# A routed MLP on one core: three transposes a slot instead of four, and list, table and list-load work in another order

## Chip, core and metric

The kernel runs on one core of one Trainium2 chip. The metric is device time in microseconds (us), the median of three runs. The profile is that of one further execution.

## The reference, cut to what matters

`x` has 8 x 2880 tokens of 192 channels. A causal convolution of 7 taps (softmaxed, one row of taps for each of 8 heads) is followed by a two-level top-1 mixture of experts with 4 x 4 = 16 experts:

```python
out = np.einsum('hk,bskhg->bshg', w, x_unf)       # the convolution
g_idx = np.argmax(x @ w_group, axis=1)            # then, for each group g:
e_idx = np.argmax(xg @ w_expert[g], axis=1)
h  = np.maximum(xg[mask_e] @ w1[g, e], 0.0)       # 192 -> 1024
ye = h @ w2[g, e]                                 # 1024 -> 192
out[tok_idx] = (g_w * e_w)[:, None] * ye          # product of the two gates
```

## The kernel before

**Units.** The 23040 tokens are convolved and routed in 18 units of 4 to 12 blocks of 120 tokens. `unit(u)` is a generator that yields between small steps. It convolves (TensorE, then ScalarE copies), turns the result, makes logits, picks the expert on VectorE, and stores gate and convolved row (193 floats) to the DRAM table `xcd`; that store is issued from ScalarE's queue (line 532). Then it builds the lists of token numbers by expert: two halves of six blocks, each with the VectorE instructions `ohl` (L567), `ohr` (L571), `ohv` (L575), then small matmuls (L589), and a scatter by GpSimd into `idtab` (L601).

**Slots.** The experts' work is a list `plan` of 98 slots of up to 256 tokens. Portion 0 is one slot for each of 16 experts (slots 0 to 15, from the first 5 units), portions 1 and 2 are two slots for each expert (16 to 47 and 48 to 79), and the tail is 18 slots whose expert is read from a table computed on the chip, nine of two tiles of 128 tokens and nine of one, in turn. For each slot two indirect DMAs of GpSimd gather rows of `xcd` into one of four buffers `xg` (L673). `turn` turns them on TensorE into the PSUM tile `px` (L686: the first 128 channels of a tile; L687: the last 64), and ScalarE and VectorE split them into a high and a low part (`xa` L688 and L689, `xb` L692 and L693). `hidden` and `back` are the two matrix products, four steps `f2` in a slot of two tiles (L704; L722 and L726), with `hh` (L709) and `hl` (L710) between them. `finish` scales the sums in the two PSUM tiles `po` into `ys` (L784, L785) and GpSimd scatters them to the output (L775). Between steps of a slot `advance` takes steps of the units.

**Order.** Each engine's order is made by a scheduler when the kernel is built. It takes an instruction as soon as its own model of time has it ready, and so far ahead of its place in the program, unless `tc.keep_in_program_order` holds it. `open_slot(i)` is called at step 0 of slot i-2; `turn` for slot i at step 1 of slot i-1 (at step 0 if that slot has one tile). `open_portion` issues the 16 loads of token lists `idp` (L1017) of a portion from the SyncE queue at once. The arithmetic of the tail's table (`table`, L824 to L907) stands at slot 52 and after in the program, one piece for each `open_slot`, then one `idpt` list load (L1035) for each. In the tail, GpSimd also does one subtraction of each expert's weights (`bl`, L647).

Of the kernel before, what the change touches and what calls it, by code (L numbers as in the profile page):

```python
# [36 lines left out]
def conv_moe_kernel(  # L37
# [18 lines left out]
    PINW = True  # L56

# [79 lines left out]
    KPRE = [2, 150, 155, 160, 162, 20]  # L137
    CEU = 0
# [226 lines left out]
    xg = [const.tile([P, 2, XW], F32, name=f"xg{i}") for i in range(NXG)]  # L365
# [10 lines left out]
    def unit(u, pre=None):  # L376
# [155 lines left out]
        SE.dma_start(out=xcw, in_=xc[0:BT, 0:nb, 0:XW])  # L532
# [28 lines left out]
        for b0 in range(0, nb, HB2):  # L561
            n = min(HB2, nb - b0)
            ohl = pa.tile([P, HB2, P], F16, name="ohl", bufs=2)
            ohr = rt.tile([P, HB2, LH], F16, name="ohr", bufs=1)
            ohv5 = pa.tile([P, HB2, LH], F16, name="ohv", bufs=2)
            bs = slice(b0, b0 + n)
            nc.vector.tensor_tensor(  # L567
                out=ohl[0:Q, 0:n], in0=iop[0:Q].unsqueeze(1).broadcast_to([Q, n, P]), in1=bc(posb[0:Q, 0, bs], P),
                op=ALU.is_equal,
            )  # L570
            nc.vector.tensor_tensor(  # L571
                out=ohr[0:Q, 0:n], in0=ior[0:Q].unsqueeze(1).broadcast_to([Q, n, LH]), in1=bc(posb[0:Q, 1, bs], LH),
                op=ALU.is_equal,
            )
            OHE.tensor_tensor(  # L575
                out=ohv5[0:Q, 0:n], in0=ohr[0:Q, 0:n], in1=bc(vals[0:Q, bs], LH), op=ALU.mult)
            halves.append((b0, n, ohl, ohv5))
# [91 lines left out]
    def gather(ids, known, n=2):  # L669
        xs = xg[nslot[0] % NXG]  # L670
        nslot[0] += 1
        for t in range(n):
            nc.gpsimd.indirect_dma_start(  # L673
                out=xs[:, t, :], out_offset=None, in_=xcd[0:known, :],
                in_offset=bass.IndirectOffsetOnAxis(ap=ids[:, t, 0:1].bitcast(U32), axis=0),
                bounds_check=known - 1, oob_is_err=False,
            )
        return xs

    def turn(xs, n=2):  # L680
# [127 lines left out]

    def table(first=None, nbig=NBIG, nsmall=NSMALL):
# [10 lines left out]
        v = nc.vector  # L820
# [23 lines left out]
        v.memset(t["one"], 1.0)  # L844
        base = cons if first is None else first
        tt(t["rem"], ends[:, nends[0]], base, ALU.subtract)
        if first is None:
# [9 lines left out]
            tt(most, most, flags[:, 0:1], ALU.max)  # L857
            ts(flags[:, 0:1], most, float(SLOT), ALU.is_gt)
            ts(flags[:, 1:2], most, float(SLOT), ALU.is_le)
            ts(t["rem"], t["rem"], flags[:, 1:2], ALU.mult)  # L860
        slots(t["nf"], P - 1 if first is None else SLOT - 1)
        slots(t["ns"], SLOT - 1)
        tt(t["ns"], t["ns"], t["nf"], ALU.subtract)
        for n, pe, st in (("nf", "pa", "sa"), ("ns", "pb", "sb")):
# [6 lines left out]

        ts(c["m1"], c["j"], float(nbig), ALU.is_ge)
# [3 lines left out]
        stt(c["ja"], c["k"], -1024.0, c["ja"], ALU.mult, ALU.add)  # L876
        stt(c["k"], c["j"], -float(ntail), c["oa"], ALU.add, ALU.is_lt)
        stt(c["k"], c["k"], 1024.0, c["oa"], ALU.mult, ALU.add)
        tt(c["k"], c["k"], c["m2"], ALU.mult)
        stt(c["jb"], c["j"], -float(nbig), c["k"], ALU.add, ALU.subtract)  # L880
        for st, pe, j, m in (("sa", "pa", "ja", "ma"), ("sb", "pb", "jb", "mb")):
# [8 lines left out]
        v.tensor_reduce(out=c["k"], in_=t["q"], axis=AX.X, op=ALU.add)  # L890
        ts(ent[:, 0:1], c["k"], float(D), ALU.mult)
        ts(ent[:, 1:2], c["k"], float(F), ALU.mult)

        ts(c["ja"], c["ja"], float(SLOT), ALU.mult, -float(DUMMY), ALU.add)
        stt(t["q"], t["sa"], -float(SLOT), base, ALU.mult, ALU.add)
        stt(t["q"], t["q"], c["ja"], t["ma"], ALU.add, ALU.mult)
        stt(t["r"], t["nf"], float(SLOT), base, ALU.mult, ALU.add)
        stt(t["r"], t["r"], -float(DUMMY), t["mb"], ALU.add, ALU.mult)
        tt(t["q"], t["q"], t["r"], ALU.add)
# [27 lines left out]
    def stages(u):  # L927
        q = units[u][1] // QB
        return 1 + 8 + (2 * FRH if u >= FRU else 0) + sum(gaps(u)) + 3 * q + 1 + (LISTLAG if u >= NEED else 0)
# [69 lines left out]

    def open_portion(pi):  # L1000
# [9 lines left out]
        else:  # L1010
# [5 lines left out]
            for e in range(E):  # L1016
                nc.sync.dma_start(  # L1017
                    out=idp[:, e],
                    in_=idtab[bass.ds(base[e], P * rows), :].rearrange("(p r) c -> p r c", r=rows),
                )  # L1020
# [42 lines left out]
    def open_slot(i):  # L1063
# [49 lines left out]
    for k in range(AHEAD):  # L1113
        step()
    while opened[0][0]["todo"]:
        split_one(opened[0][0])
    unit_banks[:] = [(pm, "pm")]
    lead[:] = SKEW2, LIVE2
    turned[0] = turn(gathered[0])
# [13 lines left out]
    for i, (pi, e, s) in enumerate(plan):  # L1133
# [7 lines left out]
        for f2 in range(steps):  # L1141
# [25 lines left out]
            if f2 == 0:  # L1167
                open_slot(i + 2)
            for q in range(f2, NF // 2, steps):
# [101 lines left out]
```

## Time and profile before

| | |
|---|---|
| median of 3 runs | 1166.22 us (1163.81 to 1169.93) |
| the profiled execution | 1157.9 us, span 1156.1 us from first to last instruction |
| granted TensorE clock, mean | 0.991 |
| TensorE (PE) busy | 1105.5 us, 96% |
| VectorE (DVE) busy | 804.7 us, 70% |
| ScalarE (ACT) busy | 689.2 us, 60% |
| GpSimd (POOL) busy | 494.2 us, 43% |

Busy times of PE are unions of pipelined matmuls: each record is longer than the distance to the next start, so the cost of one is read from starts, not from its duration. The first transposes of the slots start at 97.31 us; those that run within slot 16 (the first with the change) start at 328.66 us, within slot 48 at 686.89 us, within slot 80 (the first of the tail) at 999.80 us.

### The profile page before, as it was taken

Reading aid. Unit: us, or ns where it says so; the run is one execution under the profiler, and the core shown is the slowest. Engines: PE = TensorE matmul, PEld = TensorE weight load, DVE = VectorE, ACT = ScalarE, POOL = GpSimd, SP = SyncE. Lnnn points to the kernel's source line nnn. Section 1 sums busy time; section 2 is a strip of 40 time slices with the busy share of each in tenths; the row PEclk is TensorE's granted clock in tenths of the full one; section 3 lists DMA queues with packets and bytes.
Section 4 is the critical chain, followed back from the end, with each engine's and each line's share of the span. In section 5 each row is a group of like instructions: output and inputs, shape, how many; then the busy total and the mean of one; then the engine's idle time right before and its main releaser. Section 6 shows DMA issues by size and latency. Waiting matters only on the chain.

```text
span 1156.1 us, 23806 instructions
## 1 busy us (share of the span) xinstructions
PE 1105.5 (96%) x8468; PEld 1076.4 (93%) x8468; DVE 804.7 (70%) x1668; ACT 689.2 (60%) x1374; POOL 494.2 (43%) x443
## 2 busy tenths in 40 slices
PE   6887999989999999999999999999999999999996
PEld 5777999989999999999998999999999999989986
DVE  4777788877867666666678565666666666688874
ACT  5474666657565555655554555656555555677873
POOL 2121232435344443333344444444444445577773
PEclk9899999999999999999999999999999999999998
DMA  8869699889775554536364564544444546399970
GB/s 191 227 180 280 156 233 233 221 183 263 218 186 149 150 171 115 139 114 169 96 155 108 155 199 132 142 133 139 133 141 132 141 120 169 107 249 267 257 198 19
DMA packets 167212, 195.63 MB, mean 169 GB/s; under 512 B 22500, under 2 KB 144333, under 8 KB 167086
## 3 DMA queue, kind: packets, MB, share of 16 engines
q1 hardware_dynamic: 125006, 140.41, 46.0%
q0 software_dynamic: 18752, 35.85, 10.9%
q10 hardware_dynamic: 23328, 17.80, 6.4%
q8 instruction: 67, 1.10, 0.4%
q14 instruction: 59, 0.48, 0.1%
HBM read 158.79 MB, written 36.58 MB: 169 GB/s over the span
## 4 chain that ended last, share of the span: by engine, by line
PE 76%; DVE 8%; DMA 6%; issue 4%; ACT 3%; POOL 1%; SPq 0%; another core or an unknown queue 0%; POOLq 0%; ACTq 0%; DVEq 0%
PE ph L704 31%; PE po L722 20%; PE po L726 9%; PE pm L426 3%; PE pm L466 2%; DMA xg<-xcd,idpt 2%; PE pm L686 1%; PE pm L687 1%; DVE hl L710 1%; PE pm L445 1%; PE ph L739 1%; DVE cw L654 1%; PE pm L469 1%; DMA rawc<-in_moe_w 1%; DVE ohl L567 1%
## 5 line engine op out<-in xcount | busy, mean ns | idle before, releaser
L722 PE MATMUL po<-cw,hh 128*128 128x384 f32 x1424 | 442.3, 368 | 6.4 <-DVE ys L785 6.3
L704 PE MATMUL ph<-xa,ah 128*128 128x256 f32 x1424 | 390.1, 296 | 6.6 <-DVE xa L689 3.4
L775 POOL DMA_INDIRECT out<-ys,idp x160 | 169.2, 1057 | 449.2 <-DVE ys L785 336.6
L710 DVE SCALAR_TENSOR_TENSOR hl<-ph,hh 128x512 fp32r<-128x512 f32 x356 | 240.9, 685 | 169.9 <-ACT hh L709 155.8
L726 PE MATMUL po<-cw,hl 128*128 128x192 f32 x1424 | 356.8, 251 | 0.0
L709 ACT ACTIVATE hh<-ph 128x512 fp32r<-128x512 f32 x356 | 210.7, 594 | 212.6 <-PE ph L704 157.3
L704 PEld LDWEIGHTS ph<-xa,ah 128*128 128x128 f32 x1424 | 270.9, 190 | 9.6 <-DVE xa L689 3.6
L722 PEld LDWEIGHTS po<-cw,hh 128*128 128x128 f32 x1424 | 268.5, 189 | 10.3 <-DVE ys L785 8.2
L726 PEld LDWEIGHTS po<-cw,hl 128*128 128x128 f32 x1424 | 272.5, 191 | 1.6
L673 POOL DMA_INDIRECT xg<-xcd,idp x160 | 186.0, 1163 | 57.1 <-issue 28.7
L704 PE MATMUL ph<-xb,bh 128*128 128x256 f32 x712 | 202.0, 284 | 1.0 <-DVE xb L693 1.0
L704 PE MATMUL ph<-xb,bl 128*128 128x256 f32 x712 | 202.0, 284 | 0.0
L704 PE MATMUL ph<-xa,al 128*128 128x256 f32 x712 | 201.2, 283 | 0.0
L704 PEld LDWEIGHTS ph<-xa,al 128*128 128x128 f32 x712 | 136.5, 192 | 2.2
L704 PEld LDWEIGHTS ph<-xb,bh 128*128 128x128 f32 x712 | 136.2, 191 | 1.2 <-DVE xb L693 1.2
L704 PEld LDWEIGHTS ph<-xb,bl 128*128 128x128 f32 x712 | 136.9, 192 | 0.0
L654 DVE TENSOR_TENSOR cw<-rawc,cw 128x768 fp32r<-128x768 f32 x114 | 105.2, 953 | 14.9 <-ACT cw L653 11.9
L639 DVE TENSOR_TENSOR al<-raw,ah 128x1024 fp32r<-128x1024 f32 x57 | 70.8, 1242 | 35.8 <-ACT ah L638 19.6
L653 ACT ACTIVATE cw<-rawc 128x768 fp32r<-128x768 f32 x114 | 91.2, 839 | 3.0 <-DMA rawc<-in_moe_w 3.0
L785 DVE SCALAR_TENSOR_TENSOR ys<-po,xg,ys 128x192 f32<-128x192 f32 x187 | 76.0, 415 | 24.4 <-ACT ys L784 16.5
L692 ACT ACTIVATE xb<-pm 64x256 fp32r<-64x256 f32 x98 | 36.0, 368 | 94.8 <-DVE xa L689 89.1
L784 ACT ACTIVATE ys<-po,xg 128x192 f32<-128x192 f32 x187 | 76.1, 418 | 22.7 <-PE po L726 12.0
(223 smaller groups left out, 1552.5 us busy)
## 6 DMA issues: line engine op xcount, KB each, us to landing
rawc<-in_moe_w SPq DMA_DIRECT2D x114, 384.0 KB
raw<-in_moe_w SPq DMA_DIRECT2D x57, 512.0 KB
raw<-in_moe_w SPq DMA_DIRECT2D x114, 256.0 KB
xcd<-xc ACTq DMA_DIRECT2D x13, 1085.6 KB
xin<-in_x SPq DMA_DIRECT2D x7, 1134.0 KB
xc<-in_moe_w SPq DMA_DIRECT2D x18, 384.0 KB
xin<-in_x SPq DMA_DIRECT2D x6, 1039.5 KB
xin<-in_moe_w SPq DMA_DIRECT2D x9, 512.0 KB
```

The lines of the kernel that those rows point to most:

```text
L639: eng.get(k, nc.vector).tensor_tensor(out=al, in0=ra, in1=ah.bitcast(F32), op=ALU.subtract)
L653: pin(PINW, nc.scalar.activation(out=cw[:, fs, 0, :], in_=rc[k - 2], func=AF.Copy))
L654: eng.get(k, nc.vector).tensor_tensor(out=cw[:, fs, 1, :], in0=rc[k - 2], in1=cw[:, fs, 0, :].bitcast(F32), op=ALU.subtract,)
L673: nc.gpsimd.indirect_dma_start(out=xs[:, t, :], out_offset=None, in_=xcd[0:known, :], in_offset=bass.IndirectOffsetOnAxis(ap=ids[:, t, 0:1 ...
L704: nc.tensor.matmul(out=hp[:, j], lhsT=wgt[:, fs], rhs=xx, start=i == 0, stop=i == len(ops) - 1)
L709: nc.scalar.activation(out=hh, in_=hp, func=AF.Relu)
L710: nc.vector.scalar_tensor_tensor(out=hl, in0=hp, scalar=0.0, in1=hh.bitcast(F32), op0=ALU.max, op1=ALU.subtract,)
L722: nc.tensor.matmul(out=oo[t][:, 0:2 * D], lhsT=hh[:, j, ts], rhs=cw[:, f].rearrange("p a d -> p (a d)"), start=f == 0, stop=False,)
L726: nc.tensor.matmul(out=oo[t][:, 0:D], lhsT=hl[:, j, ts], rhs=cw[:, f, 0, :], start=False, stop=f == NF - 1,)
L775: nc.gpsimd.indirect_dma_start(out=outviews[nscat[0] % len(outviews) if view is None else view], out_offset=bass.IndirectOffsetOnAxis(ap=i ...
L784: nc.scalar.activation(out=ys[:, t, :], in_=oo[t][:, D:2 * D], func=AF.Copy, scale=g)
L785: nc.vector.scalar_tensor_tensor(out=ys[:, t, :], in0=oo[t][:, 0:D], scalar=g, in1=ys[:, t, :], op0=ALU.mult, op1=ALU.add,)
```

## The change

1. From slot 16 on (`TURN3`), a slot of two tiles has three transposes. GpSimd copies the last 64 channels of the second tile behind those of the first (`beside`, called at step 0 of the slot before), so that one transpose turns both. They come out on partitions 0 to 63 and 64 to 127 of `px`, and `xb` is made by two copies and two subtractions of 64 x 128 in place of one each of 64 x 256; for the second tile the high part lies on partitions 64 to 127. `xg` grows by 64 columns a tile.
2. From unit 8 on (`LP`) the list instructions L567, L571 and L575 are held in program order, and three yields stand between a unit's two halves.
3. The table's VectorE arithmetic is held in program order, cut by 11 more yields, and taken on also at step 2 of each slot of portion 2.
4. The 16 list loads of portions 1 and 2 are asked for in `open_slot`, two experts ahead, instead of all at once.

`SEV`, `TB` and `LG` have values that change nothing.

```diff
+    def hold(on, ins):
+        return tc.keep_in_program_order(ins) if on else ins
...
+    SEV = 99
+    TB = 0
+    HGAP = 3
+    LP = 8
+    LG = 0
+    IDN = 2
...
-    xg = [const.tile([P, 2, XW], F32, name=f"xg{i}") for i in range(NXG)]
+    xg = [const.tile([P, 2, XE], F32, name=f"xg{i}") for i in range(NXG)]
...
+            if u >= LP and b0:
+                for _ in range(HGAP):
+                    yield
...
-            nc.vector.tensor_tensor(
+            hold(u >= LP, nc.vector.tensor_tensor(
                 out=ohl[0:Q, 0:n], ...
-            OHE.tensor_tensor(
+            hold(u >= LP, OHE.tensor_tensor(
...
+    TURN3 = 16
+
+    def beside(i):
+        if i < len(plan) and i >= TURN3 and tiles(i) == 2:
+            xs = gathered[i]
+            nc.gpsimd.tensor_copy(out=xs[:, 0, XW:XE], in_=xs[:, 1, 1 + P:XW])
...
-            nc.tensor.transpose(px[0:D2, SLOT + t * P:SLOT + (t + 1) * P], xs[:, t, 1 + P:XW], ident)
+            if not three:
+                nc.tensor.transpose(px[0:D2, SLOT + t * P:SLOT + (t + 1) * P], xs[:, t, 1 + P:XW], ident)
+        if three:
+            nc.tensor.transpose(px[:, SLOT:SLOT + P], xs[:, 0, 1 + P:XE], ident)
...
+        if three:
+            for t in range(2):
+                hi, lo = slice(t * D2, (t + 1) * D2), slice((1 - t) * D2, (2 - t) * D2)
+                cs = slice(t * P, (t + 1) * P)
+                pb = px[hi, SLOT:SLOT + P]
+                nc.scalar.activation(out=xb[hi, cs], in_=pb, func=AF.Copy)
+                nc.vector.tensor_tensor(out=xb[lo, cs], in0=pb, in1=xb[hi, cs].bitcast(F32), op=ALU.subtract)
+            return xa, xb
...
+    class InOrder:
+        def __getattr__(self, name):
+            return lambda *a, **k: hold(self.on, getattr(nc.vector, name)(*a, **k))
...
-        v = nc.vector
+        v = InOrder(first is None)
...
+    def lists(pi, n):
+        while idget.get(pi) and E - len(idget[pi]) < n:
+            idget[pi].pop(0)()
...
-            for e in range(E):
-                nc.sync.dma_start(
+            idget[pi] = [lambda e=e: nc.sync.dma_start(
...
+            lists(pi, e + IDN)
...
+                beside(i + 1)
                 open_slot(i + 2)
...
+            if f2 == 2 and late and pi == len(portions) - 1 and len(idps) == len(portions):
+                next(late[0], None)
...
-                    turned[i + 1] = turn(gathered[i + 1], tiles(i + 1))
+                    turned[i + 1] = turn(gathered[i + 1], tiles(i + 1), i + 1 >= TURN3 and tiles(i + 1) == 2)
```

## Rows read from the trace of the kernel before

**Rows 1.** Busy time by stage; columns stand in the first line.

```profile
core 0: us, PE busy (x) PEld busy (x) DVE busy (x) ACT busy (x) POOL busy (x), PEclk, DMA share, GB/s
...
325.00:600.00 275.00, 273.15 (x2146) 268.38 (x2145) 184.44 (x369) 156.60 (x315) 111.43 (x100) 1.00 0.53 144
...
660.00:990.00 330.00, 330.00 (x2568) 329.99 (x2567) 210.98 (x337) 185.78 (x337) 144.05 (x136) 1.00 0.50 144
990.00:1156.10 166.10, 151.87 (x1078) 143.10 (x1076) 118.34 (x175) 117.31 (x210) 108.84 (x72) 0.98 0.72 190
```

**Rows 2.** What PE waited for: us in total, times, longest.

```profile
PE po L722 <- DVE ys L785: 6.3, 6, 1.6
...
PE ph L704 <- DVE hl L710: 3.2, 1, 3.2
...
PE pm L686 <- DMA xg<-xcd,idpt: 1.0, 3, 0.7
```

**Rows 3.** PE in order of time, slot 49: start, us, engine, line.

```profile
696.67 0.27 PE L686 MATMUL pm<-ident,xg 128*128 128x128 f32 x1
...
696.99 0.27 PE L687 MATMUL pm<-ident,xg 128*64 128x128 f32 x1
697.02 0.42 PE L722 MATMUL po<-cw,hh 128*128 128x384 f32 x1
...
701.77 0.34 PE L722 MATMUL po<-cw,hh 128*128 128x384 f32 x1
```

**Rows 4.** The instructions of tile xb: ns least/median/most, first and last start, shapes.

```profile
L692 ACT ACTIVATE xb<-pm x98: 270/377/380, 102.9 to 1133.6; 64x256 fp32r<-64x256 f32 x89, 64x128 fp32r<-64x128 f32 x9
L693 DVE TENSOR_TENSOR xb<-pm,xb x98: 283/418/420, 104.0 to 1133.9; 64x256 fp32r<-64x256 f32 x89, 64x128 fp32r<-64x128 f32 x9
```

**Rows 5.** DVE in order of time, the same slot.

```profile
699.47 0.96 DVE L785 SCALAR_TENSOR_TENSOR ys<-po,xg,ys 128x192 f32<-128x192 f32 x2
```

**Rows 6.** All waits, ACT for DVE in `turn`: total, times, longest.

```profile
ACT xb L692 <- DVE xa L689: 89.1, 91, 4.5
```

**Rows 7.** The only copy on POOL.

```profile
L359 POOL COPY wrb<-wr x1: 197/197/197, 13.4 to 13.4; 64x20 f32<-64x20 f32 x1
```

**Rows 8.** POOL in order of time: slot 50's second gather; one pair of tail slots.

```profile
684.57 1.04 POOL L673 DMA_INDIRECT xg<-xcd,idp  x1 [0.30 <-issue]
...
1085.10 1.03 POOL L673 DMA_INDIRECT xg<-xcd,idpt  x1 [0.30 <-ACT ys L784]
...
1088.52 1.46 POOL L673 DMA_INDIRECT xg<-xcd,idpt  x1 [0.30 <-ACT hh L709]
1090.00 2.42 POOL L647 TENSOR_TENSOR bl<-xin,bh 128x1024 fp32r<-128x1024 f32 x1
```

**Rows 9.** PE, the second tile's first transpose in that pair.

```profile
1089.18 0.33 PE L686 MATMUL pm<-ident,xg 128*128 128x128 f32 x1 [0.16 <-DMA xg<-xcd,idpt]
```

**Rows 10.** DVE in order of time, unit 17's lists and the table.

```profile
606.51 0.95 DVE L567 TENSOR_TENSOR ohl<-iop,posb 120x768 f16<-120x768 f32 x1
...
611.11 0.42 DVE L785 SCALAR_TENSOR_TENSOR ys<-po,xg,ys 128x192 f32<-128x192 f32 x1
```

**Rows 11.** SyncE's queue in order of time: list loads of portion 1, of the tail.

```profile
247.38 12.21 SPq L1017 DMA_DIRECT2D idp<-idtab  x16
...
642.77 11.76 SPq L1035 DMA_DIRECT2D idpt<-idtab  x14
```

**Rows 12.** ACT and its queue in order of time, at portion 1's lists.

```profile
252.15 0.32 ACTq L532 DMA_DIRECT2D xcd<-xc  x1
252.57 1.08 ACT L709 ACTIVATE hh<-ph 128x512 fp32r<-128x512 f32 x2 [7.50 <-DMA idp<-idtab]
```

**Rows 13.** DVE in order of time: what the store waited for in its data.

```profile
246.33 0.23 DVE L530 RECIPROCAL xc<-se 120x12 f32<-120x12 f32 x1
```

**Rows 14.** Busy time after that stop, columns as in rows 1.

```profile
254.00:258.00 4.00, 4.00 (x20) 3.76 (x21) 3.77 (x5) 4.00 (x7) 0.00 (x0) 0.59 0.90 206
```

**Rows 15.** The store's issues: first and last start.

```profile
L532 ACTq DMA_DIRECT2D xcd<-xc x18: 323/323/410, 23.0 to 591.0; - x18
```

More of the change, by code (lines that the diff above doesn't have):

```diff
@@ L531, in unit @@
         xcw = xcd[t0:t0 + nb * BT, :].rearrange("(b p) d -> p b d", p=BT)
-        SE.dma_start(out=xcw, in_=xc[0:BT, 0:nb, 0:XW])
+        (nc.sync if u >= SEV else SE).dma_start(out=xcw, in_=xc[0:BT, 0:nb, 0:XW])
         for _ in range(rest):
@@ L566, in unit @@
             bs = slice(b0, b0 + n)
-            nc.vector.tensor_tensor(
+            hold(u >= LP, nc.vector.tensor_tensor(
                 out=ohl[0:Q, 0:n], in0=iop[0:Q].unsqueeze(1).broadcast_to([Q, n, P]), in1=bc(posb[0:Q, 0, bs], P),
                 op=ALU.is_equal,
-            )
-            nc.vector.tensor_tensor(
+            ))
+            if u >= LP:
+                for _ in range(LG):
+                    yield
+            hold(u >= LP, nc.vector.tensor_tensor(
                 out=ohr[0:Q, 0:n], in0=ior[0:Q].unsqueeze(1).broadcast_to([Q, n, LH]), in1=bc(posb[0:Q, 1, bs], LH),
                 op=ALU.is_equal,
-            )
-            OHE.tensor_tensor(
-                out=ohv5[0:Q, 0:n], in0=ohr[0:Q, 0:n], in1=bc(vals[0:Q, bs], LH), op=ALU.mult)
+            ))
+            hold(u >= LP, OHE.tensor_tensor(
+                out=ohv5[0:Q, 0:n], in0=ohr[0:Q, 0:n], in1=bc(vals[0:Q, bs], LH), op=ALU.mult))
             halves.append((b0, n, ohl, ohv5))
@@ L673, in gather @@
             nc.gpsimd.indirect_dma_start(
-                out=xs[:, t, :], out_offset=None, in_=xcd[0:known, :],
+                out=xs[:, t, 0:XW], out_offset=None, in_=xcd[0:known, :],
                 in_offset=bass.IndirectOffsetOnAxis(ap=ids[:, t, 0:1].bitcast(U32), axis=0),
@@ L678, in gather, with turn @@
         return xs
-    def turn(xs, n=2):
+    TURN3 = 16
[3 more added lines that the diff above has]
+            nc.gpsimd.tensor_copy(out=xs[:, 0, XW:XE], in_=xs[:, 1, 1 + P:XW])
+    def turn(xs, n=2, three=False):
         px = pm.tile([P, 512], F32, name="pm")
@@ L844, in table @@
         v.memset(t["one"], 1.0)
+        yield
         base = cons if first is None else first
@@ L857, in table @@
             tt(most, most, flags[:, 0:1], ALU.max)
+            yield
             ts(flags[:, 0:1], most, float(SLOT), ALU.is_gt)
@@ L861, in table @@
         slots(t["nf"], P - 1 if first is None else SLOT - 1)
+        yield
         slots(t["ns"], SLOT - 1)
         tt(t["ns"], t["ns"], t["nf"], ALU.subtract)
+        yield
         for n, pe, st in (("nf", "pa", "sa"), ("ns", "pb", "sb")):
@@ L890, in table @@
         v.tensor_reduce(out=c["k"], in_=t["q"], axis=AX.X, op=ALU.add)
+        yield
         ts(ent[:, 0:1], c["k"], float(D), ALU.mult)
@@ L894, in table @@
         ts(c["ja"], c["ja"], float(SLOT), ALU.mult, -float(DUMMY), ALU.add)
+        yield
         stt(t["q"], t["sa"], -float(SLOT), base, ALU.mult, ALU.add)
         stt(t["q"], t["q"], c["ja"], t["ma"], ALU.add, ALU.mult)
+        yield
         stt(t["r"], t["nf"], float(SLOT), base, ALU.mult, ALU.add)
         stt(t["r"], t["r"], -float(DUMMY), t["mb"], ALU.add, ALU.mult)
+        yield
         tt(t["q"], t["q"], t["r"], ALU.add)
@@ L1015, in open_portion @@
             )
-            for e in range(E):
-                nc.sync.dma_start(
-                    out=idp[:, e],
-                    in_=idtab[bass.ds(base[e], P * rows), :].rearrange("(p r) c -> p r c", r=rows),
-                )
+            idget[pi] = [lambda e=e: nc.sync.dma_start(
+                out=idp[:, e],
+                in_=idtab[bass.ds(base[e], P * rows), :].rearrange("(p r) c -> p r c", r=rows),
+            ) for e in range(E)]
         idps[pi] = idp
@@ L1112, in conv_moe_kernel @@
         pre[e] = weights(e * D, e * F)
-    for k in range(AHEAD):
+    for k in range(AHEAD - TB):
         step()
@@ L1116, in conv_moe_kernel @@
         split_one(opened[0][0])
+    if TB:
+        turned[0] = turn(gathered[0])
+    for k in range(TB):
+        step()
     unit_banks[:] = [(pm, "pm")]
     lead[:] = SKEW2, LIVE2
-    turned[0] = turn(gathered[0])
+    if not TB:
+        turned[0] = turn(gathered[0])
     pinned[0] = False
```

8 lines of the change are left out of this document (7 added, 1 removed).

## The prediction, made before the change was timed

> **What bounds the kernel.** I read busy time by stage first, then what TensorE waited for, then single slots in order of time. From 660 to 990 us PE is busy for all of the 330 us, at granted clock 1.00, and from 325 to 600 us for 273.15 of 275, while DVE has a third of its time free and ACT and POOL more [rows 1]. The reader is to see that in slots 16 to 79 whatever is taken off PE shortens the span, and that work added elsewhere is free until it is late. The tail is different: 14 us of its 166 are without PE work, and DVE, ACT and POOL are busy for 65 to 71% of it. Second, PE's waits are few: 6.3 us in 6 for `ys`, 3.2 us once for `hl`, 1.0 us in 3 for a gather of the tail [rows 2]. These are all that a better order of DVE, ACT or loads can give back, plus what the clock loses after a stop.
>
> **One transpose fewer.** 64 slots (16 to 79) and nine tail slots lose one, 73 in all. The four start from 696.67 to 696.99 [rows 3]: 0.107 us apart (0.32 over three), though each record lasts 0.27. The following matmul starts 0.03 us after the last. What one gives back thus lies between 0.03 (if only the last, overlapped place goes) and 0.107; a start in the middle of the row goes, so I take 0.107. 73 x 0.107 = 7.8 us, 6.8 of it in slots 16 to 79, where PE is the bound. By the low end it would be 2.2.
>
> The Trainium skill ("TensorE: Matmul & The Clock Gate", Part 4: PE-mode transpose) gives about 275 ns for such a transpose within a kernel, most of it access latency. By that figure 73 would give an estimated 20 us; the trace's durations agree with it (0.27), but its starts, 0.107 apart, say that the latency is overlapped, and they decide.
>
> **The longer hand-over in `turn`.** One ACT copy of 64 x 256 (377 ns) becomes two of 64 x 128 (270 each, by the nine of the tail), one DVE subtraction (418) two of 283 [rows 4]: +0.16 us of ACT and +0.15 of DVE a slot, 12 us each over 73 slots, in time that both have free. What can matter is the sequence. ACT waited for DVE's `xa` before `xb` 91 times, 89.1 us [rows 6], though both only read `px`: the two take turns on that tile. If the second tile takes its turn after the first, ACT's `ys`, queued behind on ACT, and with it DVE's, is later by one copy and one subtraction, 0.27 + 0.28, plus two hand-overs and less the shorter first pair: 0.5 us, at most 0.8. In slot 49 `ys` ends at 700.43 (699.47 + 0.96) [rows 5] and PE first needs its PSUM tile at 701.77 [rows 3]: 1.34 us are left, so the steady slots pay nothing. Six slots had nothing left [rows 2]; one or two that stay so pay 0.5 to 0.8 each. I take +1.0, ends 0 and 4.8 (six times 0.8).
>
> The Trainium skill ("PSUM — Partial Sum Buffer", PSUM bank collisions raise a hardware error) says that two engines may use one bank at the same time in different 32-partition quadrants; the two tiles now lie on partitions 0 to 63 and 64 to 127. By it the second pair need not wait, and the term would be an estimated 0.4. The waits of rows 6 are on the same quadrants, so they can't tell the two readings apart.
>
> **The copy on POOL.** The nearest row is a copy of 64 x 20 in 197 ns [rows 7]; the far one a subtraction of 128 x 1024 in 2.42 us [rows 8]. 128 x 64 is nearer the first: 0.3 us. In slots 16 to 79 a gather is issued a slot and more before its turn (slot 50's second ends its issue at 685.61, its turn starts at 696.67 [rows 3, 8]), and since POOL then waits for the next `ys`, the copy is done long before. Not in the tail: there the second gather ends its issue at 1086.13 (1085.10 + 1.03), its data land at about 1089.1, where PE's transposes of that tile waited 0.16 [rows 8, 9]. The copy can start only then. On POOL the next gather and `bl` come at that time too [rows 8]; the third transpose can't start before about 1089.5, while the last of today's four follows 0.11 behind the start at 1089.18 [rows 9]. If the copy is ahead of the gather of 1088.52, POOL stands for about 0.7 us and PE is late by 0.2 to 0.4. If it is behind that gather, which ends at 1089.98, PE is late by about 1.2; behind `bl` (to 1092.42) by 3.5. I take 0.3, nine times: +2.7; ends 0 and 31.5.
>
> **DVE's bursts.** From 606.51 to 611.11 DVE went through unit 17's six list instructions and the first of the table's arithmetic, which stands at slot 52 in the program but ran from slot 39 on [rows 10]; `ys` of that slot came at 611.11 and PE had stopped. Five of the six waits for `ys` follow such a burst of L567 or of the table; the sixth and longest, 1.6, an ACT delay [rows 2]. Holding spreads lists by three yields a unit, and puts the table into slots that have 36% of DVE free [rows 1]. Of 6.3 - 1.6 = 4.7 us I take 3.7 as gained (one such wait stays); ends 4.7 and -2, if a held instruction stands in DVE's queue before an `hl` that PE needs.
>
> **List loads.** At 247.38 SyncE began 16 loads that took 12.21 us [rows 11]. The store of unit 12's rows, ready in its data at 246.56 [rows 13], was issued from ACT's queue only at 252.15, and ACT stood 7.50 us, released by one of those loads [rows 12]. `hl` came late, PE stopped 3.2 us [rows 2], and ran the next 4.0 us at a granted clock of 0.59, that is mostly at the lower of the two levels (1.2 GHz) [rows 14]: 1.6 us more. Price 4.8 us. Against a gain: loads asked for one by one over many slots need not run so; 14 of the tail's, one a slot in the program, ran together [rows 11], since nothing holds them. But the stop needs a store in the burst, and from 252.15 to 591.0 there are six (units 12 to 17), 68 us apart [rows 12, 15]; a burst of 12.21 us catches one by chance in 18%, and three more yields a unit shift them against each other. I take 4.8 as gained, ends 4.8 and 0. What is moved behind: the first list of a portion is now asked for two slots before use, behind five weight loads on SyncE; its gather is issued at step 0 of slot 14 and turned at step 1 of slot 15, so a load late by up to a slot costs nothing; the price of a later one is one stop of PE for each portion, which I leave in the upper end.
>
> **Sum.** -7.8 + 1.0 + 2.7 - 3.7 - 4.8 = -12.6 us. On the profiled execution (span 1156.1, 1.8 around it) that gives 1157.9 - 12.6 = 1145.3. The runs' median is 8.3 above that execution, which no row explains; taking that as unchanged, 1166.2 - 12.6 = 1153.6.
>
> **Rivals.** (a) Only the transposes count: the loads still collide and the bursts only move. -7.8 + 1.0 + 2.7 = -4.1: 1162; with half of the orders' gain, 1158. For it: the tail's list loads, which ran together. (b) The tail's copy: if POOL has it behind `bl` in each of nine pairs, 9 x 3.5 = 31.5 in place of 2.7, 1182. From 1.7 us late in each (15.3 of the other terms over nine) the change is no longer a gain. Behind the gather alone (9 x 1.2 = 10.8) it is 1162. For it: POOL goes from that gather straight to `bl` [rows 8]; against: the copy stands ahead of that gather in the program. (c) Held instructions stall DVE: 20 halves of lists at up to 0.5 us, +10 in place of -3.7: 1167. Against: their inputs come from DVE itself just before. (d) A transpose is worth its 0.27 us: 73 x 0.27 = 19.7, 1142; the starts speak against it.
>
> **Chances.** Forecast 0.48, itself 1148 to 1158; (a) 0.22; (b) behind `bl` 0.07, behind the gather 0.10; (c) 0.06; (d) 0.07. The range 1145 to 1164 leaves out (d), the first (b) and part of (c). 0.5% is 5.8 us, about what a measurement of this kernel tells from none: faster means below 1160.4. Faster: the forecast, (d), half of (a) and some of (b): 0.70. Same: the rest of (a) and (b) behind the gather, part of (c): 0.20. Slower: 0.10.
>
> **What would show it.** Starts of `turn` in a steady slot: three, 0.107 apart, and each slot shorter by that. PE's waits: `ys` one or two left, the stop at 250 gone. In the tail: a wait of L686 or its successor for POOL's copy, with its size. The forecast fails if PE's steady slots don't shorten by 0.1, if the copy stands behind `bl`, or if PE stops for `hl` behind held lists.

## The result, and the profile after

The changed kernel takes 1150.22 us (median of 4 runs, 1148.39 to 1152.3), the kernel before on the same chip 1165.01 (4 runs, 1158.92 to 1169.93): ratio 0.9888, 95% interval 0.9842 to 0.9934. The profiled execution took 1149.03 us, its span is 1147.3; before they were 1157.9 and 1156.1. Forecast were 1153.6, range 1145 to 1164. The span of the profiled pair fell by 8.8 us, the medians by 14.8.

First the busy time by stage of the changed kernel, as in [rows 1], with the bounds moved to its earlier tail.

```profile
core 0: us, PE busy (x) PEld busy (x) DVE busy (x) ACT busy (x) POOL busy (x), PEclk, DMA share, GB/s
...
660.00:975.00 315.00, 315.00 (x2447) 315.00 (x2446) 212.66 (x413) 179.26 (x357) 162.55 (x163) 1.00 0.50 142
975.00:1147.30 172.30, 154.40 (x1068) 143.99 (x1066) 129.66 (x184) 119.45 (x219) 113.12 (x83) 0.97 0.68 184
```

PE is still busy without a break up to 975, on 75 instructions a slot in place of 76; the tail has grown (table below). Next, what PE waited for (total, times, longest), the rows that answer to [rows 2].

```profile
PE po L799 <- DVE hl L785: 4.3, 7, 1.0
...
PE po L756 <- DVE ys L819: 1.6, 4, 0.6
PE po L793 <- DVE ys L819: 1.5, 4, 0.7
```

The single stop of 3.2 us for `hl` is gone, and `ys` waits fell from 6.3 to 1.6 us (L756 is the former L722). All 4.3 us of the first row and the 1.5 us of the last lie in the tail. Before, PE waited there for `hl` already, at what was then L765:

```profile
PE po L765 <- DVE hl L751: 3.1, 8, 0.6
```

Then PE in order of time in a steady slot, the answer to [rows 3].

```profile
684.86 0.38 PE L709 MATMUL pm<-ident,xg 128*128 128x128 f32 x2
685.08 0.27 PE L713 MATMUL pm<-ident,xg 128*128 128x128 f32 x1
685.11 0.42 PE L756 MATMUL po<-cw,hh 128*128 128x384 f32 x1
```

And the instructions of the third transpose's line from 700 to 770 us (count, ns least/median/most, first and last start):

```profile
L713 PE MATMUL pm<-ident,xg x7: 272/272/273, 704.4 to 762.4; 128*128 128x128 f32 x7
```

Three transposes, 0.11 apart, and the next matmul 0.03 behind the last. Seven of them span 58.0 us, six slots of 9.667. Before, a steady slot took 9.778 us.

To see where time came from, I cut the span at the first matmul on `hh` and `cw` of slots 8, 16, 48 and 79, read off PE in order of time. The last column runs from there to the end of the last scatter's issue on POOL, 7.8 us ahead of the span's end (8.2 with the lists without yields and holding).

| profiled execution of | slots 8 to 16 | 16 to 48 | 48 to 79 | tail |
|---|---|---|---|---|
| before | 101.55 | 357.27 | 303.13 | 153.23 |
| changed kernel | 93.88 | 349.03 | 299.67 | 159.63 |
| orders alone | 94.09 | 351.12 | 303.13 | 153.63 |
| transposes alone | 101.16 | 358.05 | 300.81 | 160.10 |
| three transposes up to slot 79 only | 93.09 | 349.01 | 300.83 | 153.06 |
| list loads at once | 97.72 | 349.30 | 299.67 | 160.30 |
| lists without yields and holding | 98.83 | 358.00 | 301.29 | 159.16 |
| lists' yields, lists not held | 94.97 | 349.38 | 299.67 | 158.59 |
| table not held | 93.09 | 353.92 | 299.67 | 163.15 |
| tail copies made, not used | 93.09 | 349.28 | 299.82 | 162.21 |
| tail copy later on POOL | 93.09 | 349.53 | 299.67 | 161.75 |
| tail copy on ACT | 93.09 | 349.27 | 306.54 | 199.83 |
| tail `bl` on DVE | 95.17 | 349.09 | 299.67 | 157.25 |
| five gather buffers | 93.01 | 348.77 | 299.59 | 166.59 |

The change took 19.4 us from the first three columns and gave 6.4 back in the tail: -13.0. The stretch up to slot 8 is not in the table; in the same two executions it was 4.1 us longer after, and it varied by up to 7 us between the kernels of the table, though none is meant to change the work there.

### The profile page after: what moved, and what is told of

The parts are those of the page before. It is cut to its first block, busy times and chain, and to the rows that moved or that the text cites. A ratio compares the mean times of both kernels' runs of the same rounds, so it can differ in the third digit from the quotient of the medians.

```text
span 1147.3 us, 23858 instructions
## 1 busy us (share of the span) xinstructions
PE 1100.9 (96%) x8395; PEld 1070.5 (93%) x8395; DVE 822.6 (72%) x1741; ACT 696.2 (61%) x1447; POOL 536.3 (47%) x516
## 4 chain that ended last, share of the span: by engine, by line
PE 80%; DVE 8%; issue 5%; ACT 3%; DMA 2%; POOL 1%; POOLq 0%; DVEq 0%; ACTq 0%; SPq 0%
PE ph L738 33%; PE po L756 21%; PE po L760 10%; PE pm L436 4%; PE pm L476 3%; DMA xcd<-xc 2%; PE pm L709 1%; PE pm L455 1%; DVE hl L744 1%; DVE al L655 1%; PE pm L479 1%; ACT ah L654 1%; DVE cw L670 1%; PE pm L713 1%; PE ph L436 1%
## 5 line engine op out<-in xcount | busy, mean ns | idle before, releaser
L756 PE MATMUL po<-cw,hh 128*128 128x384 f32 x1424 | 442.3, 368 | 1.6 <-DVE ys L819 1.6
L756 PEld LDWEIGHTS po<-cw,hh 128*128 128x128 f32 x1424 | 268.4, 188 | 4.8 <-DVE ys L819 2.8
L809 POOL DMA_INDIRECT out<-ys,idp x160 | 184.6, 1154 | 178.6 <-DVE ys L819 103.1
L689 POOL DMA_INDIRECT xg<-xcd,idp x160 | 191.8, 1199 | 55.9 <-issue 40.6
L701 POOL COPY xg<-xg 128x64 f32<-128x64 f32 x73 | 24.1, 330 | 222.5 <-DMA xg<-xcd,idp 202.7
L670 DVE TENSOR_TENSOR cw<-rawc,cw 128x768 fp32r<-128x768 f32 x114 | 107.9, 976 | 18.1 <-ACT cw L669 15.2
L655 DVE TENSOR_TENSOR al<-raw,ah 128x1024 fp32r<-128x1024 f32 x57 | 79.7, 1398 | 30.9 <-ACT ah L654 26.3
L722 ACT ACTIVATE xb<-pm 64x128 fp32r<-64x128 f32 x146 | 39.6, 271 | 87.0 <-DVE xa L715 57.6
L819 DVE SCALAR_TENSOR_TENSOR ys<-po,xg,ys 128x192 f32<-128x192 f32 x187 | 71.8, 413 | 23.9 <-ACT ys L818 19.9
```

The costliest lines, as they stand in the source:

```text
L655: eng.get(k, nc.vector).tensor_tensor(out=al, in0=ra, in1=ah.bitcast(F32), op=ALU.subtract)
L670: eng.get(k, nc.vector).tensor_tensor(out=cw[:, fs, 1, :], in0=rc[k - 2], in1=cw[:, fs, 0, :].bitcast(F32), op=ALU.subtract,)
L689: nc.gpsimd.indirect_dma_start(out=xs[:, t, 0:XW], out_offset=None, in_=xcd[0:known, :], in_offset=bass.IndirectOffsetOnAxis(ap=ids[:, t, ...
L756: nc.tensor.matmul(out=oo[t][:, 0:2 * D], lhsT=hh[:, j, ts], rhs=cw[:, f].rearrange("p a d -> p (a d)"), start=f == 0, stop=False,)
L809: nc.gpsimd.indirect_dma_start(out=outviews[nscat[0] % len(outviews) if view is None else view], out_offset=bass.IndirectOffsetOnAxis(ap=i ...
L819: nc.vector.scalar_tensor_tensor(out=ys[:, t, :], in0=oo[t][:, 0:D], scalar=g, in1=ys[:, t, :], op0=ALU.mult, op1=ALU.add,)
```

## Experiments: the orders

**Each half by itself.** One kernel keeps four transposes everywhere, the other keeps the old order of lists, table and list loads:

```
-    TURN3 = 16
+    TURN3 = 999
```

and, for the transposes alone, lists neither yielded nor held, the table not held, all 16 list loads as a portion opens, and the last portion's extra step of late work (at `f2 == 2`) gone; the table's 11 more yields stay:

```
-    LP = 8
+    LP = 99
...
-        v = InOrder(first is None)
+        v = nc.vector
...
+        lists(pi, E)
```

> The changed kernel with four transposes in every slot and no copy on POOL (xg keeps its new width). Theory A: slots 48 to 79 at 9.778 us, the tail as before (153 us from slot 79's first back to the end), no stop at 250 us and no more than two waits for ys: 8 to 9 us faster than before. Theory B: within 3 us of before.

> The changed kernel with list and table instructions, yields at step 2 and list loads as they were before; the three transposes and POOL's copy stay. Theory A (the parts add up): slots 48 to 79 at 9.667 us as in the changed kernel, 64 x 0.111 = 7.1 us less there, the tail 6 us longer than before, the stop at 250 us and the six waits for ys still there: 0 to 3 us faster than before. Theory B (the orders give nothing, their stops only move by chance): as fast as the changed kernel, some 13 us faster than before.

Measured against the same runs of the kernel before: orders alone 1148.65 us, ratio 0.9888 (0.9854 to 0.9922); transposes alone 1166.92, 1.0043 (1.0021 to 1.0066). So the orders make as much as the whole change, and the transposes without them make the kernel 0.4% slower, in an interval that leaves out 1. In the profile the columns up to slot 79 gain 1.9 us and the tail loses 6.9. PE's waits from 200 to 990 us, with the transposes alone:

```profile
PE po L756 <- DVE ys L819: 9.3, 10, 1.8
PE ph L738 <- DVE hl L744: 3.9, 2, 3.0
```

and with the orders alone:

```profile
PE po L756 <- DVE ys L819: 0.2, 1, 0.2
```

With the orders alone almost nothing of [rows 2] is left in these slots. With the transposes alone, the steady slots are as short as in the changed kernel (9.667), but in slots 16 to 48, where 32 x 0.111 = 3.5 us should come off, 0.8 came on: PE waits for `ys` ten times for 9.3 us instead of six for 6.3, and behind the wait at 612 us the granted clock was 0.59 from 613 to 617, 1.6 us more. My reading is that the second pair of `xb` copies makes `ys` later, and that PE pays for it where DVE bursts have already used the room. In these profiles the two halves of the change are not independent; the times alone don't show it, since 0.9888 x 1.0043 = 0.993 lies in the changed kernel's interval.

**List loads.** The lists of a portion are asked for as it opens, everything else as changed:

```
+        lists(pi, E)
```

> The changed kernel with the 16 list loads of a portion issued at once, as before. Theory A (spreading the loads in the program takes the stop at 250 us away): ACT stands some 7 us behind the loads at portion 1's opening, PE stops about 3 us and the kernel is 4 to 5 us slower than the changed one. Theory D (the three yields a unit shifted the store against the burst, the loads run in one burst either way): no stop, same time as the changed one.

Measured 1150.2 us, ratio 0.9908 (0.9874 to 0.9941). The interval holds the changed kernel's ratio, so the time alone settles little. The profile tells more: slots 8 to 16 are 3.8 us longer than in the changed kernel. SyncE's queue there, then ACT, in order of time:

```profile
249.57 11.30 SPq L1076 DMA_DIRECT2D idp<-idtab  x16
260.96 0.95 SPq L642 DMA_DIRECT2D rawc<-in_moe_w  x2
...
265.34 0.84 ACT L669 ACTIVATE cw<-rawc 128x768 fp32r<-128x768 f32 x1 [5.61 <-DMA rawc<-in_moe_w]
```

The burst is back, 16 loads in 11.30 us. The store that was caught in it before [rows 12] went out at 245.50, ahead of the burst, because the yields had shifted the two. This time the weights `rawc` were caught, queued on SyncE behind the loads; ACT stood 5.61 us, and PE stopped 2.3 us for `hl`, after which its granted clock was 0.82 and 0.75 in the two stretches of 4 us from 265. In the changed kernel two loads go out at that place, three more 68 us later:

```profile
249.16 2.81 SPq L1076 DMA_DIRECT2D idp<-idtab  x2
316.75 1.39 SPq L1076 DMA_DIRECT2D idp<-idtab  x3
...
613.04 10.35 SPq L1076 DMA_DIRECT2D idp<-idtab  x8
```

They are not spread one by one, eight still run together at 613, but no wait of PE follows there. The yields are not needed against the old stop either: with the lists without yields (next) and the loads spread, the store went out at 244.50 behind two loads, and PE did not stop there.

**Yields or holding.** Three kernels take parts of the new order of lists and table away. The first has the lists without yields and not held, the table as changed:

```
-    LP = 8
+    LP = 99
```

The second keeps all yields. It was meant to hold nothing, and its expectation says so, but `hold` now acts on `None` alone and the table hands it `None`: the lists are let go, and the table is still held:

```
-        return tc.keep_in_program_order(ins) if on else ins
+        return tc.keep_in_program_order(ins) if on is None else ins
...
-            self.on = on
+            self.on = None if on else False
```

The third keeps all yields, holds the lists, but not the table:

```
-        v = InOrder(first is None)
+        v = nc.vector
```

> The changed kernel with unit 8's and later list instructions not held and without the three yields between halves (LP = 99); table and loads as changed. Theory A (bursts of lists cost the waits for ys): four or five waits for ys are back, 0.4 to 1.6 us each, and the kernel is 3 to 6 us slower than the changed one; the store of unit 12 goes out after portion 1's first loads again, but only two loads are ahead of it, so no stop at 250 us. Theory G (holding doesn't matter, the table alone made the bursts): same time, no more than two such waits.

> The yields of the lists and of the table and the three more stages a unit stay, nothing is held in program order. Theory A (holding is what counts): DVE's order lets list and table instructions run in bursts again, `ys` waits of 4 us or more and a stop for `hl` with 3.4 us at the lower clock once or twice: span 1152 to 1158, ratio 0.994 to 1.0, near the kernel with the lists not held. Theory B (spreading by yields is what counts): span 1145 to 1149, ratio 0.987 to 0.991.

> Lists are held as in the changed kernel, the table's arithmetic has its yields but is not held. Theory A (the lists' holding made the gain, the table's burst was worth one `ys` wait of about 1.5 us): span 1147 to 1150, ratio 0.988 to 0.992. Theory B (the table's burst made half of it): `ys` waits of 3 us or more between slots 37 and 55, span over 1151, ratio over 0.992.

Measured: lists without yields and holding 1155.39 us, 1.0001 (0.9985 to 1.0018); lists' yields with only the table held 1145.76, 0.9918 (0.9888 to 0.9949); table not held 1149.27, 0.9951 (0.9928 to 0.9975). Without the lists' yields and holding the whole gain in time is gone, though loads are spread and the table is held. PE's waits there, 200 to 990 us:

```profile
PE po L756 <- DVE ys L819: 6.3, 6, 1.8
PE ph L738 <- DVE hl L744: 2.3, 2, 1.3
```

Two of those stops were followed by stretches in which the clock fell. Busy time of that kernel, columns as in [rows 1]:

```profile
294.00:298.00 4.00, 4.00 (x23) 4.00 (x21) 4.00 (x6) 3.93 (x8) 3.21 (x2) 0.57 0.76 229
355.00:359.00 4.00, 3.46 (x16) 3.46 (x17) 3.95 (x8) 0.00 (x0) 3.39 (x3) 0.59 0.25 74
```

With the lists' yields and the lists not held, the stages are those of the changed kernel to within 1.1 us, and one `ys` wait of 1.7 us came back. The six list instructions of a unit start within 3.5 to 4.3 us of each other without yields, within 3.6 to 4.9 with them, and within 4.9 to 9.0 when also held. So it is spreading the lists over more stages that pays; that holding the lists adds anything is not shown.

Holding the lists and not the table cost 4.9 us in slots 16 to 48, in a profiled execution that was the slowest of twelve (1155.11); in time the intervals of the second and third kernel overlap. In two of those slots, 2.7 us longer together, the table's instructions ran side by side from 600 to 610 us on DVE, and PE paid:

```profile
600.98 0.44 PE L756 MATMUL po<-cw,hh 128*128 128x384 f32 x1 [1.61 <-DVE ys L819]
...
612.83 0.44 PE L756 MATMUL po<-cw,hh 128*128 128x384 f32 x1 [0.98 <-DVE ys L819]
```

Most of the rest is in two slots in which PE waited 1.3 us for a gather. One instruction of the table shows where it stands (count, ns, start): first with the lists let go and the table held, then with the table let go.

```profile
L849 DVE TENSOR_TENSOR most<-most,flags x1: 159/159/159, 683.4 to 683.4; 128x1 f32<-128x1 f32 x1
L871 DVE TENSOR_TENSOR most<-most,flags x1: 159/159/159, 599.3 to 599.3; 128x1 f32<-128x1 f32 x1
```

In the changed kernel it starts at 684.2. So it is holding the table that keeps it spread. A kernel with all yields and nothing held was not run.

## Experiments: the copy in the tail

**Four transposes in the tail.** No copy and no third-transpose form from slot 80 on:

```
-        if i < len(plan) and i >= TURN3 and tiles(i) == 2:
+        if i < tail0 and i >= TURN3 and tiles(i) == 2:
...
-  turned[i + 1] = turn(gathered[i + 1], tiles(i + 1), i + 1 >= TURN3 and tiles(i + 1) == 2)
+  turned[i + 1] = turn(gathered[i + 1], tiles(i + 1), TURN3 <= i + 1 < tail0)
```

> The changed kernel with three transposes in slots 16 to 79 alone; the tail's slots turn with four and without a copy on POOL. Theory A (the tail's 6 us were lost to the copy, which makes POOL stand until the gather has landed and pushes its bl onto DVE's al): the tail is 153 to 154 us again and the kernel 4 to 6 us faster than the changed one. Theory C (the tail is longer because table and lists come later): the tail stays at 159 us.

Measured 1140.47 us, ratio 0.982 (0.9796 to 0.9845): the best version. Orders alone (0.9888) and list loads at once (0.9908), measured beside it, have intervals that lie above its own; the changed kernel's (0.9842 to 0.9934), measured apart from it, touches it. Its tail is 6.6 us shorter than the changed kernel's.

In the changed kernel POOL, in order of time in one pair of tail slots, reads (the answer to [rows 8]):

```profile
1058.32 1.03 POOL L689 DMA_INDIRECT xg<-xcd,idpt  x1 [0.30 <-ACT ys L818]
1061.67 0.72 POOL L701 COPY xg<-xg 128x64 f32<-128x64 f32 x1 [2.32 <-DMA xg<-xcd,idpt]
1062.55 1.02 POOL L809 DMA_INDIRECT out<-ys,idpt  x1 [0.16 <-issue]
1063.88 1.03 POOL L689 DMA_INDIRECT xg<-xcd,idpt  x1 [0.30 <-issue]
1064.93 2.40 POOL L663 TENSOR_TENSOR bl<-xin,bh 128x1024 fp32r<-128x1024 f32 x1
1067.83 2.85 POOL L663 TENSOR_TENSOR bl<-raw,bh 128x1024 fp32r<-128x1024 f32 x1 [0.50 <-ACT bh L662]
```

and DVE beside it:

```profile
1061.08 1.22 DVE L655 TENSOR_TENSOR al<-xin,ah 128x1024 fp32r<-128x1024 f32 x1
...
1065.73 2.69 DVE L655 TENSOR_TENSOR al<-raw,ah 128x1024 fp32r<-128x1024 f32 x1 [0.82 <-ACT ah L654]
1068.45 0.69 DVE L785 TENSOR_TENSOR hl<-pm,hh 128x512 fp32r<-128x512 f32 x1
```

The copy stands directly behind its own gather, ahead of the next scatter and gather, so POOL waits 2.32 us for the data to land. The next gather and `bl` follow later, `bl` then runs at the same time as DVE's `al`, and `al` takes 2.69 us in place of 1.22; `hl` behind it and `ys` behind that are late. Of PE's 4.3 us for `hl` (L799) only some 1.2 are new against the 3.1 of before; its 1.5 us for `ys` (L793) are new, and so is a wait of 0.9 for `bl` in the first pair of tail slots. That pair took 19.4 us against 16.1 with four transposes, and in it the granted clock was 0.67 from 1002 to 1006. PE itself waits for the copy 0.2 us, here in the pair of the rows above:

```profile
1062.45 0.33 PE L713 MATMUL pm<-ident,xg 128*128 128x128 f32 x1 [0.20 <-POOL xg L701]
```

Over the tail the eight `al` from `raw` of the changed kernel:

```profile
L655 DVE TENSOR_TENSOR al<-raw,ah 128x1024 fp32r<-128x1024 f32 x8 | 19.8, 2472 | 6.5 <-ACT ah L654 6.5
```

and with four transposes in the tail:

```profile
L655 DVE TENSOR_TENSOR al<-raw,ah 128x1024 fp32r<-128x1024 f32 x8 | 10.0, 1251 | 8.4 <-ACT ah L654 8.4
```

**Copies made, not used.** The tail's copies stay on POOL, its turns use four transposes:

```
-  turned[i + 1] = turn(gathered[i + 1], tiles(i + 1), i + 1 >= TURN3 and tiles(i + 1) == 2)
+  turned[i + 1] = turn(gathered[i + 1], tiles(i + 1), TURN3 <= i + 1 < tail0)
```

> The changed kernel; in the tail POOL still copies the second tile's last channels, but the slot turns with four transposes and nothing reads the copy. Theory A (POOL stands for the gather and pushes what is behind it, so that bl runs with DVE's al): the tail is still 158 to 160 us, al of the tail's big slots still above 2 us, though no transpose waits for the copy. Theory E (the loss is the third transpose's own wait for the copy): the tail is 153 to 154 us, as with four transposes and no copy.

Measured 1147.34 us, ratio 0.9918 (0.9887 to 0.9949); tail 162.21, in the slowest of five executions (1150.49). Seven of the eight `al` from `raw` are long again, two of them 5.63 us, and PE waits 6.1 us in three for `ys`:

```profile
L655 DVE TENSOR_TENSOR al<-raw,ah 128x1024 fp32r<-128x1024 f32 x8 | 25.6, 3206 | 8.3 <-ACT ah L654 8.3
```

Nobody reads these copies, and neither tail nor time is better for it. The third transpose and its wait are not needed for the cost; the copies on POOL are enough.

**`bl` on DVE.** The tail's `bl` leave POOL, the copies stay:

```
-  *tail_regs(lambda c: tab[0][0:1, j, c:c + 1], 2), {1: nc.gpsimd}, spare=(i - tail0) % 2 == 0)
+  *tail_regs(lambda c: tab[0][0:1, j, c:c + 1], 2), {}, spare=(i - tail0) % 2 == 0)
```

> The changed kernel with the tail's bl subtraction on DVE in place of POOL. Theory A, if the overlap of bl with al is most of the loss: al is 1.2 us again, DVE has 1.2 us more a slot, and the tail is 153 to 157 us. If POOL's standing costs in another way (late gathers): al 1.2 us and the tail 158 us or more.

Measured 1143.53 us, ratio 0.99 (0.9873 to 0.9927); tail 157.25. `al` from `raw` is back at 1226 ns on average and the waits for `hl` L785 are gone, though POOL still stands for its gathers. In their place PE waits for a DVE that now has `bl` too:

```profile
PE po L793 <- DVE ys L819: 8.1, 8, 1.3
```

**A later place on POOL.** The copy is put behind the opening of the next slot and held there; in the built order it stands behind the next scatter and gather, ahead of `bl`:

```
-            nc.gpsimd.tensor_copy(out=xs[:, 0, XW:XE], in_=xs[:, 1, 1 + P:XW])
+            hold(i >= tail0, nc.gpsimd.tensor_copy(out=xs[:, 0, XW:XE], in_=xs[:, 1, 1 + P:XW]))
...
             if f2 == 0:
-                beside(i + 1)
+                if i + 1 < tail0:
+                    beside(i + 1)
                 open_slot(i + 2)
+                if i + 1 >= tail0:
+                    beside(i + 1)
```

> In the tail alone the copy of the second tile's last channels stands behind the next scatter and gather on POOL, still ahead of `bl`, and is held there. Theory (POOL's standing for its own gather's landing, 1.7 to 2.6 us a pair, pushes `bl` into DVE's `al` and that is what the tail lost): the copy finds its data landed or nearly so, the standing falls under 0.5 us a pair, `al` is back near 1.24 us, the third transpose waits up to 1 us where the gather took long; tail 154 to 157 us in place of 159.6, ratio to before 0.984 to 0.987. Rival (that there is a copy between gather and third transpose is the cost, wherever it stands): tail stays 159 to 162, ratio 0.988 to 0.992. The prediction's own price for this place, 1.2 us a pair, would give 11 us more than four transposes: tail 164.

Measured 1144.73 us, ratio 0.9919 (0.989 to 0.9948); tail 161.75. POOL in order of time, and PE:

```profile
1036.40 1.45 POOL L689 DMA_INDIRECT xg<-xcd,idpt  x1 [0.30 <-issue]
1037.85 0.25 POOL L701 COPY xg<-xg 128x64 f32<-128x64 f32 x1
1038.06 2.40 POOL L663 TENSOR_TENSOR bl<-xin,bh 128x1024 fp32r<-128x1024 f32 x1
...
1038.15 0.33 PE L713 MATMUL pm<-ident,xg 128*128 128x128 f32 x1 [1.29 <-POOL xg L701]
```

The first half of my theory held: the copy waits for nothing, takes 0.25 us, and `al` is back at 1226 ns. The time did not follow: PE now waits for the copy, 8.9 us in 7 waits of up to 1.3. The tail is no better than with POOL standing, as the rival said. This is the prediction's case "behind the gather", priced at 1.2 us a pair; 8.9 / 7 = 1.27.

**On ACT.** In the tail ACT makes the copy instead of POOL; its built place is behind `hh` of the one-tile slot.

```
-            nc.gpsimd.tensor_copy(out=xs[:, 0, XW:XE], in_=xs[:, 1, 1 + P:XW])
+            if i < tail0:
+                nc.gpsimd.tensor_copy(out=xs[:, 0, XW:XE], in_=xs[:, 1, 1 + P:XW])
+            else:
+                nc.scalar.activation(out=xs[:, 0, XW:XE], in_=xs[:, 1, 1 + P:XW], func=AF.Copy)
```

> In the tail alone ACT makes the copy, in its order right behind `hh` of the one-tile slot and ahead of the next `hh`. Theory (POOL's order is what cost): POOL goes from its gather straight on to scatter, gather and `bl` as before the change, `bl` and `al` no longer run together, tail 153 to 157 us, ratio 0.983 to 0.987. Rival (whoever stands for the landing costs it): ACT waits 1 to 2 us for the gather in front of the next `hh` in every pair, PE waits for `hl` or `ys` instead, tail 160 or more, ratio 0.99 or more.

Measured 1190.43 us, ratio 1.032 (1.0286 to 1.0355); tail 199.83. ACT and POOL, in order of time:

```profile
1032.09 0.26 ACT L704 ACTIVATE xg<-xg 128x64 f32<-128x64 f32 x1 [7.21 <-DMA xg<-xcd,idpt]
...
1028.93 1.03 POOL L689 DMA_INDIRECT xg<-xcd,idpt  x1 [0.30 <-issue]
1035.10 1.00 POOL L812 DMA_INDIRECT out<-ys,idpt  x1 [5.14 <-DVE ys L822]
```

ACT began to stand 4 us before the gather was issued (1032.09 - 7.21 against 1028.93), 56.1 us over 8 such waits in the tail. Meanwhile the `ys` of the next scatter, which needs ACT, was late, and POOL waited 5.14 us for it. PE waited 28.7 us for `ys` in this tail, at a granted clock of 0.91. The rival won by far: on ACT the standing costs more than on POOL.

**Five buffers.** A fifth gather buffer, the two tiles packed to make room (all reads of `xs` go by a helper that gives the same columns):

```
-    NXG = 4
-    xg = [const.tile([P, 2, XE], F32, name=f"xg{i}") for i in range(NXG)]
+    NXG = 5
+    xg = [const.tile([P, XE + XW], F32, name=f"xg{i}") for i in range(NXG)]
```

> The changed kernel with five gather buffers in place of four (laid out without the second tile's unused columns), so that the tail's gathers are issued a slot earlier and have landed when POOL comes to the copy. Theory A: the copy starts at once, POOL doesn't stand, the tail is 152 to 154 us and the kernel 6 to 9 us faster than the changed one, as fast as with four transposes in the tail or 1 us faster. Theory F (any copy among POOL's work in the tail costs the same): the tail stays at 158 to 160 us.

Measured 1153.99 us, ratio 1.0001 (0.9978 to 1.0025). The copy still stands behind its own gather, and once that took long. POOL in order of time:

```profile
1001.16 0.23 POOL L706 COPY xg<-xg 128x64 f32<-128x64 f32 x1 [5.98 <-DMA xg<-xcd,idpt]
```

what PE waited for:

```profile
PE ph L743 <- POOL bl L668: 8.4, 1, 8.4
```

and the busy time behind it, columns as in [rows 1]:

```profile
1002.00:1010.00 8.00, 6.25 (x28) 6.26 (x29) 1.38 (x2) 1.19 (x2) 7.08 (x5) 0.52 0.08 23
```

`bl` stood behind that copy, PE stopped 8.4 us, and in the 8 us that followed its granted clock was 0.52. This one stop makes most of the long tail (the first pair took 28.1 us, the others 16.4 to 17.0), but the twelve runs are no faster than before either. The fifth buffer does not help while the copy follows its gather in POOL's order.

## Why the prediction came out, by its own steps

The total of 1153.6 against 1150.2 is right, but that is partly luck: two terms were wrong by 5 and 6 us, and they cancelled. For the profiled execution the forecast was 1145.3 against 1149.03; most of that miss is the stretch up to slot 8, 4.1 us longer after, which the forecast left as it was. From the table, against -12.6 in the forecast:

| term | forecast | measured | how |
|---|---|---|---|
| transposes | -7.8 | -8.1 | 73 x 0.111 |
| longer hand-over | +1.0 | +1.5 | slots 16 to 48: 349.03 - 351.12 + 32 x 0.111 |
| copy on POOL, tail | +2.7 | +7.6 | tail: 159.63 - 153.06 + 9 x 0.111 |
| DVE bursts | -3.7 | -9.8 | orders alone, slots 8 to 48: 94.09 + 351.12 - 101.55 - 357.27 = -13.6, less the loads |
| list loads | -4.8 | -3.8 | slots 8 to 16: 93.88 - 97.72 |

These sum to -12.6, to the tenth by chance: they are differences of single profiled executions, and the columns of the two kernels themselves give -13.0. One stop by chance shifts such a row: with four transposes in the tail, slots 48 to 79 took 300.83 in place of 299.67, 0.9 of it in a slot in which PE waited for a gather.

**The transposes** were sized right: 9.778 to 9.667 us a slot. The row that showed it was the distance of starts, not the duration (0.27); rival (d) is out. In the nine slots of the tail the 0.111 is assumed.

**The hand-over** was sized right, under its condition. ACT's second copy does take its turn after DVE's first subtraction. The instructions of `xb` in the changed kernel, and ACT's wait, answer to [rows 4, 6]:

```profile
L722 ACT ACTIVATE xb<-pm x146: 260/272/275, 318.7 to 1115.1; 64x128 fp32r<-64x128 f32 x146
L723 DVE TENSOR_TENSOR xb<-pm,xb x146: 283/290/296, 319.3 to 1115.4; 64x128 fp32r<-64x128 f32 x146
```

```profile
ACT xb L722 <- DVE xb L723: 20.3, 57, 0.5
```

0.36 us a wait. The two pairs lie on different partitions; that ACT waits all the same I put down to the order built for one tile, which no run here tests. PE pays in four small waits for `ys`, 1.6 us, where the orders alone have one of 0.2: not the one or two of 0.5 to 0.8 that I priced. (DVE's longer work comes to 11 us over 73 slots, not 12; nothing hangs on it.) In slots 16 to 79 the copy on POOL was free, as forecast, though POOL stood 202.7 us for gathers there.

**The copy on POOL** is the step that failed. I took 0.3 us a pair from PE's side, the third transpose being that much later, and that was about right: PE waited 0.2 for it, in four pairs. What I left out was what is queued behind the copy on POOL. "POOL stands for about 0.7 us" was too little: the copy came ahead of the scatter as well, right behind its own gather, POOL stood 1.6 to 3.9 us, and `bl` moved into `al`. That `al` and `bl` hinder each other is in the rows: `bl` runs from 1064.93 to 1067.33, `al` starts at 1065.73 and ends at 1068.42, 1.09 us after `bl`, which is nearly its own 1.22. It is as if it began when `bl` ended. Seven of the eight `al` that met such a `bl` in this tail end 1.09 us after it, and the two `al` of 5.63 us with the unread copies stood through two `bl` and end 1.09 us after the second. The copy shows the same from the other side: it took 1.32 us where it started together with an `al`, and 0.24 in the median of 73. POOL and DVE at that place, in order of time:

```profile
1044.07 1.32 POOL L701 COPY xg<-xg 128x64 f32<-128x64 f32 x1 [1.73 <-DMA xg<-xcd,idpt]
...
1044.07 1.22 DVE L655 TENSOR_TENSOR al<-xin,ah 128x1024 fp32r<-128x1024 f32 x1
```

The Trainium skill ("SBUF — State Buffer", Who interferes with whom) says that a VectorE instruction with two SBUF inputs contends with a GpSimd instruction that reads SBUF, and that what they share is locked exclusively; the trace agrees, by the 1.09 us. The trace of before had it too: four of its `al` in the tail met the last 0.2 to 0.6 us of a `bl`, took 1.30 to 1.65 us and end 1.09 us after it. And that `bl` takes 2.4 us [rows 8] and follows the copy was there to be read. How much of the 7.6 us the meeting of `al` and `bl` makes is not shown apart: with `bl` on DVE the tail is 157.25, but DVE then has more to do. No place that was tried had the cost back: ahead of the next gather POOL stands, behind it PE waits 8.9 us, and on ACT it is far worse. A copy on VectorE was not run.

**DVE's bursts** were mis-sized: with the orders alone one `ys` wait of 0.2 us is left of the 6.3 us, where I had taken 3.7 as gained, and each wait had cost more than its record. Before, the wait of 1.58 us at 323 us put PE's next start 1.95 us behind its usual time. The six come to 7.5 us by starts; what is left of the 9.8, some 2 us, I can't name. I had also booked the longest, an ACT delay, as untouched; it went with the new order.

**List loads** were sized right. The -3.8 is what spreading gives once the yields have moved the store. With the orders alone, the slot that had the stop took 11.97 us in place of 16.78: 4.8, as priced, and booked so the bursts come to 8.8. The changed kernel's store and clock at that place, answering to [rows 12, 14]:

```profile
245.77 0.32 ACTq L542 DMA_DIRECT2D xcd<-xc  x1
```

```profile
250.00:254.00 4.00, 4.00 (x29) 3.78 (x28) 4.00 (x5) 2.84 (x5) 2.69 (x3) 1.00 0.90 202
254.00:258.00 4.00, 4.00 (x31) 3.89 (x30) 2.27 (x5) 2.46 (x6) 0.00 (x0) 1.00 1.05 283
```

No stop and no loss of clock. The picture of how was incomplete: either part alone takes the store out of the burst, the spread loads (store at 244.50 without yields) or the yields (245.50 with all loads at once), but with the yields alone the weights are caught instead. I had said that a stop needs a store in the burst; a load that PE will need soon does as well. Rival (a) is out. Of (c) there is no sign: PE has no wait for `hl` in the changed kernel's slots 16 to 79.

## What to carry to other kernels

When an instruction is added to an in-order queue behind a transfer, price what stands behind it on that queue, not only who waits for its result. A saving on the engine that sets the pace holds only where its hand-over has room, so look for the waits already at zero room before adding to the chain ahead of them. A total that comes out is no proof of its terms; a kernel for each half of the change was what found the better version, with the copy left out of the tail.

## What was not expected of the hardware

In the tail an indirect gather of 128 rows landed 1.6 to 6.0 us after its issue ended (POOL's waits at the copy, 3.9 at most in the changed kernel and 5.98 with five buffers). `al` on DVE and `bl` on POOL, both on 128x1024 operands, don't slow each other gradually: `al` ends 1.09 us after the `bl` that it met, however early it began (2.69 in place of 1.22 us, 5.63 behind two), and this shows in no wait of either engine. After stops of PE of under 2 us the granted clock fell in places (0.57 and 0.59 over 4 us in the windows above), which about doubles what such a stop costs; after the one of 1.58 us in the kernel before it did not.
